# Attention followed by a gated feed-forward on one core: the loads of w3 and w_out first, four partial sums of their product held in the score buffers, dummy matmuls, and a new model and queue rule for the static order

## Chip, cores and metric

The kernel runs on one core of one Trainium2 chip. The metric is the device time of one execution in microseconds (us); lower is better. A time is about 1.7 us longer than the span that the profile of the same execution shows, so spans are compared with spans and times with times. TensorE is called PE below, ScalarE ACT, VectorE DVE, GpSimd POOL and SyncE SP, as the profile calls them.

## The reference

Sliding-window attention with four sink keys, then a multiplicative feed-forward without a nonlinearity:

```python
# q, k, v: [4 batches, 8 heads, 768 positions, 64];  n_sink 4, window 128
scores = q @ k.T / sqrt(64)
keep   = (key < 4) | (0 <= query - key < 128)
x      = softmax(where(keep, scores, -1e9)) @ v      # as [3072 tokens, 512]
a, b   = x @ w1, x @ w2                              # w1, w2: [512, 1024]
out    = ((a * b) @ w3) @ w_out                      # w3: [1024, 1024], w_out: [1024, 512]
```

All inputs are float32 in memory; the loads convert them to bfloat16 on the way.

## The kernel before

There is nothing nonlinear between `w3` and `w_out`, so the kernel multiplies them once ("the fold", `w3o = w3 @ w_out`) and then has only one product per token block. The fold needs 64 transposes of `w3` blocks and a product of 1024 x 1024 x 512. It uses nothing of q, k or v, so it can run while those are still being loaded.

All loads are issued by GpSimd, in one fixed order. `("w3", 2, 4)` is row blocks 2 and 3 of `w3`, `("wo", 0)` the left half of the columns of `w_out`, `("qkv", 0, 0, 2)` blocks 0 and 1 of k, q and v of batch 0:

```python
order = [("w3", 0, 1), ("wo", 0), ("w3", 1, 2), ("qkv", 0, 0, 2), ("w3", 2, 4), ("w1", 0), ("w2", 0),
         ("qkv", 0, 2, 4), ("wo", 1), ("w3", 4, 6), ("w1", 1), ("w2", 1), ("qkv", 0, 4, 6),
         ("w3", 6, 8), ("qkv", 1, 0, 6), ("qkv", 2, 0, 6), ("qkv", 3, 0, 6)]
# ... load(*order[0]), identity; then order[1:4]
# ... five affine_selects on GpSimd build the masks here
for x in order[4:]:
    load(*x)
```

The fold works by row block and half of the columns, so each matmul has 256 columns:

```python
def fold_mm(i, n):
    po = ps_mm.tile([P, DM // 2], FP32, tag="mm", name="pw")
    cols = slice(n * DM // 2, (n + 1) * DM // 2)
    for j in range(KFF):                          # KFF = 8
        nc.tensor.matmul(po[:], w3T[i][:, j, :], wo_sb[:, j, cols],
                         start=(j == 0), stop=(j == KFF - 1))
    yield
    nc.scalar.copy(w3o[:, i, cols], po[:])
```

The order of instructions on PE, ACT, DVE and SP is static. While the program is built, a small simulation decides it: it guesses when each load arrives, how long each task takes, and picks for each engine what to put next. Its guesses don't change what is computed, only the order in which each engine must do it:

```python
arrive, clock = {}, 2.2
def lands(key, us): ...                    # clock += us; arrive[key] = clock
# q, k, v block: 0.95 us each, and arrive + 3.0;  w3 row block: 1.5;  half of w1, w2, w_out: 3.0
...
URGENT = {"g": 0, "av": 0, "sc": 2}        # ACT and DVE: among what is ready, the most urgent first
```

Score tiles live in two buffers (`ps_sc`, `bufs=2`) of PSUM, the memory that PE writes its results to. Output tiles `o_sb` live in three SBUF buffers, and SP carries both the output stores and, for batches 2 and 3, the transposes of q and k by DMA.

The softmax here doesn't subtract the row's maximum and nothing guards it: scores larger than these inputs give would overflow.

## Time and profile before

| | before |
|---|---|
| time, median of the first three runs | 215.45 us (215.21 to 215.82) |
| span of the profiled run (its time 214.53 us) | 212.8 us |
| PE busy | 92% of the span |
| last fold matmul ends | 57.6 us |
| last of all weights and of batch 0 landed | 46.7 us |
| last load landed | 112.4 us |

The page of the profile gives busy time by engine, then the span in 40 equal slices with the busy share in tenths and the clock that was granted to PE, then the chain of waits followed back from the last instruction:

```profile
PE 195.3 (92%) x1888; PEld 131.8 (62%) x1888; DVE 109.5 (51%) x258; ACT 110.4 (52%) x197; POOL 75.0 (35%) x97
...
PE   0287799999998999999999999999999999999993
...
PEclk9999969999999999999999999999999999999998
...
PE 86%; POOL 5%; DMA 3%; DVE 3%; issue 1%; ACT 1%; POOLq 0%; ACTq 0%; DVEq 0%
```

PE is full from the sixth slice on. What is to be had lies in the first five slices (each 5.3 us), where PE shows 0, 2, 8, 7, 7 tenths. The view of waits says what PE waited for: total us, number of waits, longest:

```profile
PE tp_232 L301 <- DMA w_sb<-in_moe_w_dram: 5.1, 1, 5.1
PE pw L313 <- DMA wo_sb<-in_moe_w_out_dram: 3.8, 1, 3.8
PE tp_304 L301 <- DMA w_sb<-in_moe_w_dram: 1.4, 1, 1.4
PE xt L269 <- DVE xn L259: 1.2, 3, 0.6
```

The view by windows gives, for each stretch, its length and the busy time (with instruction count) of PE, PE's weight loads, DVE, ACT and POOL; then the granted clock, and two columns on DMA that are not used here:

```profile
0.00:10.00 10.00, 1.11 (x9) 0.95 (x10) 4.50 (x10) 1.28 (x1) 8.80 (x17) 1.00 0.85 110
10.00:20.00 10.00, 7.77 (x70) 6.22 (x71) 3.27 (x9) 1.33 (x3) 9.20 (x13) 1.00 1.75 183
20.00:30.00 10.00, 8.07 (x82) 5.55 (x77) 5.73 (x17) 5.58 (x10) 6.36 (x8) 0.86 1.90 178
30.00:37.00 7.00, 6.94 (x76) 5.76 (x75) 3.32 (x7) 3.54 (x8) 2.13 (x4) 0.95 1.22 207
37.00:60.00 23.00, 23.00 (x320) 20.51 (x316) 15.05 (x33) 13.78 (x29) 19.40 (x24) 1.00 2.27 163
60.00:85.00 25.00, 24.18 (x332) 19.92 (x333) 20.12 (x53) 17.51 (x33) 18.64 (x23) 1.00 2.21 149
```

Up to 37 us PE is busy for 1.11 + 7.77 + 8.07 + 6.94 = 23.9 us. The clock column needs care: before the first clock record it shows full speed. The first record in the trace, at 17.03 us, is the change *to* full speed. The durations agree with that. The timeline of PE lists start, length, instructions, and the idle time before them with what ended it:

```profile
5.07 1.03 PE L301 MATMUL tp_232<-ident,w_sb 128*128 128x128 bf16 x8 [5.07 <-DMA w_sb<-in_moe_w_dram]
9.92 1.87 PE L313 MATMUL pw<-wo_sb,w3t 128*128 128x256 bf16 x8 [3.82 <-DMA wo_sb<-in_moe_w_out_dram]
...
27.02 5.10 PE L284 MATMUL pg<-xT_102,w_sb 128*128 128x256 bf16 x30 [0.46 <-ACT xT_102 L271]
32.85 1.04 PE L313 MATMUL pw<-wo_sb,w3t 128*128 128x256 bf16 x8
```

Eight fold matmuls of one shape took 1.87 us at 9.92 us and 1.04 us at 32.85 us. The 30 gate matmuls at 27.02 us fell into a second stretch of half clock, recorded from 27.27 to 30.69 us.

### The profile page before, as it was taken

To read this page: it belongs to the slowest core of one execution; us is meant where nothing else is said; L and a number is where in the kernel's file an instruction comes from. 1 tells how busy PE (TensorE), PEld (TensorE's weight loads), DVE (VectorE), ACT (ScalarE), POOL (GpSimd) and SP (SyncE) were. 2 spreads that over 40 slices of the span, in tenths; PEclk is the share of its full clock that TensorE was granted. 3 is DMA by queue.
4 is the path that set the end of the run, shared out by engine and by line. 5 is a ranking of instruction groups with operands and counts; after the bars stand their busy time and mean duration, and the time that the engine had idled before them with its cause. 6 is when DMAs were issued, how large, how long until landed. Compare 5 with 4: busy or idle time off the path is not lost.

```text
span 212.8 us, 4647 instructions
## 1 busy us (share of the span) xinstructions
PE 195.3 (92%) x1888; PEld 131.8 (62%) x1888; DVE 109.5 (51%) x258; ACT 110.4 (52%) x197; POOL 75.0 (35%) x97
## 2 busy tenths in 40 slices
PE   0287799999998999999999999999999999999993
PEld 0266468998987887666666555666664466554441
DVE  7116825836697787776776444687740044440000
ACT  2012636644866686786666766766643333323332
POOL 7996573679999665666000000000000000000000
PEclk9999969999999999999999999999999999999998
DMA  4999999999999999999996222100002310002343
GB/s 65 160 170 205 165 198 204 163 178 157 156 155 132 156 156 149 136 154 146 140 117 124 102 107 93 49 2 3 0 3 99 148 49 3 2 0 99 152 162 133
DMA packets 96710, 24.43 MB, mean 115 GB/s; under 512 B 88496, under 2 KB 92592, under 8 KB 96688
## 3 DMA queue, kind: packets, MB, share of 16 engines
q0 software_dynamic: 80176, 14.69, 89.5%
q1 hardware_dynamic: 16512, 9.44, 21.3%
q8 instruction: 15, 0.25, 0.5%
q14 instruction: 7, 0.06, 0.1%
HBM read 29.36 MB, written 6.29 MB: 168 GB/s over the span
## 4 chain that ended last, share of the span: by engine, by line
PE 86%; POOL 5%; DMA 3%; DVE 3%; issue 1%; ACT 1%; POOLq 0%; ACTq 0%; DVEq 0%
PE pg L284 41%; PE po L323 20%; PE av L253 7%; PE sc L222 6%; PE pw L313 6%; DMA w_sb<-in_moe_w_dram 3%; PE xt L269 3%; PE sp L202 2%; PE tp L168 1%; POOL vN_90 L101 1%; POOL qN_82 L101 1%; DVE xn L259 1%; POOL kN_86 L101 1%; DVE am L231 1%; POOL w_sb L108 1%
## 5 line engine op out<-in xcount | busy, mean ns | idle before, releaser
L284 PEld LDWEIGHTS <-w_sb 128*128 128x128 bf16 x576 | 54.2, 99 | 27.6 <-issue 3.4
L227 ACT ACTIVATE ex<-sc 128x1024 bf16<-128x1024 f32 (+1 forms) x48 | 44.3, 955 | 13.3 <-PE sc L222 13.0
L291 ACT COPY a_sb<-pg 128x384 f32<-128x384 f32 (+1 forms) x72 | 32.1, 446 | 34.2 <-PE pg L284 20.0
L231 DVE TENSOR_TENSOR am<-ex,maskt 128x1024 bf16<-128x1024 bf16 (+1 forms) x48 | 30.4, 643 | 10.0 <-ACT ex L227 9.0
L327 ACT COPY o_sb<-po 128x512 f32<-128x512 f32 x24 | 14.0, 585 | 27.2 <-PE po L323 24.8
L284 PE MATMUL pg<-xT_102,w_sb 128*128 128x256 bf16 x192 | 26.6, 285 | 1.1 <-DVE kT_99 L171 0.6
L284 PE MATMUL pg<-xT_103,w_sb 128*128 128x384 bf16 x128 | 23.8, 326 | 0.0
L284 PE MATMUL pg<-xT_104,w_sb 128*128 128x384 bf16 x128 | 23.0, 326 | 0.0
L313 PE MATMUL pw<-wo_sb,w3t 128*128 128x256 bf16 x128 | 17.3, 291 | 4.6 <-DMA wo_sb<-in_moe_w_out_dram 3.8
L259 DVE TENSOR_TENSOR xn<-av,rec 128x256 bf16<-128x256 f32 x48 | 20.4, 425 | 1.7
L284 PE MATMUL pg<-xT_105,w_sb 128*128 128x384 bf16 x128 | 21.0, 326 | 0.0
L288 DVE TENSOR_TENSOR ab_109<-a_sb,pg 128x384 bf16<-128x384 f32 x16 | 8.9, 555 | 22.3 <-PE pg L284 22.3
L253 PEld LDWEIGHTS <-am 128*128 128x128 bf16 x352 | 16.7, 97 | 2.9 <-DVE am L231 1.1
L313 PEld LDWEIGHTS <-w3t 128*128 128x128 bf16 x128 | 12.5, 103 | 7.4 <-issue 3.1
L257 DVE RECIPROCAL rec<-av 128x4 f32<-128x4 f32 x48 | 8.6, 179 | 14.9 <-PE av L253 14.8
L316 ACT CAST w3o<-pw 128x256 bf16<-128x256 f32 x16 | 5.8, 379 | 18.0 <-PE pw L313 17.9
L288 DVE TENSOR_TENSOR ab_106<-a_sb,pg 128x256 bf16<-128x256 f32 x24 | 10.0, 417 | 9.7 <-PE pg L284 9.7
L288 DVE TENSOR_TENSOR ab_108<-a_sb,pg 128x384 bf16<-128x384 f32 x16 | 8.8, 552 | 5.8 <-PE pg L284 5.4
L323 PE MATMUL po<-w3o,ab_106 128*128 128x512 bf16 x48 | 11.4, 380 | 0.0
L269 PE MATMUL xt<-ident,xn 128*128 128x128 bf16 x96 | 9.7, 220 | 1.2 <-DVE xn L259 1.2
L323 PE MATMUL po<-w3o,ab_107 128*128 128x512 bf16 x48 | 10.7, 379 | 0.0
L323 PE MATMUL po<-w3o,ab_108 128*128 128x512 bf16 x48 | 10.7, 379 | 0.0
(129 smaller groups left out, 261.3 us busy)
## 6 DMA issues: line engine op xcount, KB each, us to landing
out_dram<-o_sb SPq DMA_DIRECT2D x24, 256.0 KB, 2.0
w_sb<-in_moe_w_dram POOLq DMA_DIRECT2D x7, 512.0 KB, 9.8
wo_sb<-in_moe_w_out_dram POOLq DMA_DIRECT2D x2, 512.0 KB, 8.8
kN_86<-in_k_dram POOLq DMA_DIRECT2D x6, 128.0 KB, 10.8
qN_82<-in_q_dram POOLq DMA_DIRECT2D x6, 128.0 KB, 10.7
vN_90<-in_v_dram POOLq DMA_DIRECT2D x6, 128.0 KB, 9.9
kN_87<-in_k_dram POOLq DMA_DIRECT2D x6, 128.0 KB, 7.2
qN_83<-in_q_dram POOLq DMA_DIRECT2D x6, 128.0 KB, 6.6
```

Of the source, the lines that this page charges most:

```text
L222: nc.tensor.matmul(sc[:, e, c:c + n], kT[b][hp, r, kb * P:(kb + 1) * P], qT[b][hp, r, qb * P:qb * P + n], start=True, stop=True)
L227: nc.scalar.activation(ex[:, :, c0:], sc[:, :, c0:], ACTF.Exp, scale=scale)
L231: nc.vector.tensor_mul(am[:, :, c0:], ex[:, :, c0:], mk)
L253: nc.tensor.matmul(o, lhs, rhs, start=(n == 0), stop=(n == len(todo) - 1), skip_group_check=True)
L259: nc.vector.tensor_mul(xn[:], av[:, :, :, 0:D], rec[:].to_broadcast([P, 2, 2, D]))
L269: nc.tensor.transpose(xt[:, r, i, :], xn[:, i, :, :].rearrange("p e d -> p (e d)"), ident[:])
L284: nc.tensor.matmul(pg[:], w_sb[:, kk, dt * P:(dt + 1) * P], xT[b][:, kk, tk], start=(kk == 0), stop=(kk == NP - 1))
L288: nc.vector.tensor_mul(ab[b][:, dt, tk], gate_a.pop((b, c, dt))[:], pg[:])
L291: nc.scalar.copy(a_sb[:], pg[:])
L313: nc.tensor.matmul(po[:], w3T[i][:, j, :], wo_sb[:, j, cols], start=(j == 0), stop=(j == KFF - 1))
L323: nc.tensor.matmul(po[:], ab[b][:, kk, m * P:(m + 1) * P], w3o[:, kk, :], start=(kk == 0), stop=(kk == KFF - 1))
L327: nc.scalar.copy(o_sb[:], po[:])
```

## The change

The intent is to give PE useful work while q, k and v are still on their way: load `w3` and `w_out` almost first, start the fold on half of `w_out`, fill what idle time is left with dummy matmuls that keep the clock up, and tell the scheduling model how loads really land, as one first-in-first-out queue.

Cut to its core (`...` marks cuts; in the last lines numbers from several lines are put into one, and the comments are mine):

```diff
+    SPLIT = 4
...
-    order = [("w3", 0, 1), ("wo", 0), ("w3", 1, 2), ("qkv", 0, 0, 2), ("w3", 2, 4), ("w1", 0), ("w2", 0),
-             ("qkv", 0, 2, 4), ("wo", 1), ("w3", 4, 6), ("w1", 1), ("w2", 1), ("qkv", 0, 4, 6), ...
+    order = [('w3', 2, 4, 1, 2), ('w3', 0, 1, 0, 1), ('w3', 1, 2, 0, 1), ('w3', 3, 4, 0, 1),
+             ('w3', 2, 3, 0, 1), ('wo', 0), ('w3', 0, 2, 1, 2), ('wo', 1), ('w3', 6, 8, 0, 2),
+             ('w3', 4, 5, 0, 2), ('qkv', 0, 0, 2), ('qkv', 0, 2, 4), ('w3', 5, 6, 0, 2), ('w1', 0),
+             ('w2', 0), ('w2', 1), ('w1', 1), ('qkv', 0, 4, 6), ('qkv', 1, 0, 6), ...
...
+    def fold_mm(i, j0, j1):
+        if i >= SPLIT:
+            po = ps_mm.tile([P, DM], FP32, tag="mm", name="pw")[:]
+        else:                                      # rows 0..3: held in the two score buffers
+            if i % 2 == 0 and j0 == 0:
+                held[i // 2] = ps_sc.tile([P, 2, DM], FP32, tag="sc", name="ph")
+            po = held[i // 2][:, i % 2, :]
+        for j in range(j0, j1):
+            nc.tensor.matmul(po, w3T[i][:, j, :], wo_sb[:, j, :],
                              start=(j == 0), stop=(j == KFF - 1))
...
+    def keep_busy(n):
+        pz = ps_mm.tile([P, 512], FP32, tag="mm", name="pz")
+        for _ in range(n):
+            nc.tensor.matmul(pz[:], idle[:, 0:P], idle[:, 0:512], start=True, stop=True)
...
-    clock = 2.2           # q/k/v 0.95 (+3.0 to arrive), w3 row block 1.5, other weights 3.0
+    LAG, clock = 1.5, 2.8 # q/k/v 0.87 (+0.75 beside DMA transposes), w3 half row block 0.64, others 2.57
+    XP_US = 7.5           # a DMA transpose, to landing; was 6.5
...
-    URGENT = {"g": 0, "av": 0, "sc": 2}               # rank among what is ready
+    YIELD = {"g": 0.0, "av": 0.0, "sc": 0.4}          # us that a task lets others go first
```

In the new order `w_out` is loaded by half of its rows, so a matmul of the fold has all 512 columns. The first four row blocks can accumulate over the first half of the inner dimension as soon as the first half of `w_out` is there, and finish with the second half. In between, their partial sums stay in the two score buffers.

## The prediction

> **What bounds the kernel now.** TensorE. The busy table gives PE 92% of the 212.8 us span (ScalarE 52%, VectorE 51%); the chain of waits is 86% PE. By windows, PE is nearly full from 31 us to 209 us. The loss is the start: in 0:35 us PE is busy 21.9 us, part of it at half clock. The waits view gives 5.1 us until the first w3 block lands, 3.8 us for w_out's first half, 1.4 us for w3 blocks 2 and 3. The clock records show half speed until 17.0 us and again from 27.3 to 30.7 us (32 gate matmuls there took 5.8 us; at the later pace of 109 ns they take 3.5).
>
> The loads are a queue that never empties: they land in the order of issue, 2.5 us apart per 512 KB of weights and 0.87 us per 128 KB of q, k or v, until all weights and batch 0 are in at 46.7 us. The change moves the same bytes, so that moment stays; only what PE does meanwhile can change.
>
> **What the change does.**
> 1. It loads w3 and w_out almost first. 3 MB (15 us of queue) buys 64 transposes (56 ns each) and all fold matmuls.
> 2. Fold matmuls are 64 of 512 columns, not 128 of 256: by the projection's pace (216 ns against 110 ns) 13.8 us instead of 14.1. Four row blocks accumulate half by half in the score buffers, so they start on half of w_out. PSUM copies: 8 of 0.59 us instead of 16 of 0.38; off the chain.
> 3. 29 dummy matmuls fill idle time and warm the clock. The Trainium skill ("TensorE: Matmul & The Clock Gate", Part 1) says the clock is throttled until about 3.4 us of activity; this trace agrees that it is half until 17.0 us of sparse work.
> 4. The fold ends early, so projections of batch 0 become a stock of ready PE work.
>
> **Cost.** The first four small loads are followed on GpSimd by four mask operations (about 2.4 us in this trace), so the queue should run dry for about 2 us around 6 to 8 us. I estimate w_out's halves landing near 12.2 and 16 us, batch 0's second key pair at 30 us, the first gate weights complete near 37 us. By then the changed kernel will have done about 23.7 us of useful PE work (fold 17.4, attention of two blocks 6.3); the kernel before had done about 17.0. With the fold's 0.3 us that is a lead of about 7 us. Part goes back: the third block of q and k lands about 3 us later than before (44 to 47 us), and the changed order asks for it near 44 us; I expect 1.5 to 2.5 us of load waits in 40 to 62 us. Before lost about 4 us after 37 us; I expect much the same in total. After 62 us PE should be full, with the same 40 us tail.
>
> **Predicted time: 208.3 us** (205.0 to 212.0). Faster by over 2%: 0.82; within 2%: 0.16; slower: 0.02.
>
> **What would show it.** Clock full from 5 to 7 us on, with no second dip; PE waiting on w_out near 12 us; last fold matmul near 35 us (before 57 us); gates starting near 37 us; load waits on kN and qN near 44 us; spacing of loads unchanged; PE over 97% busy from 62 us on.
>
> **What would make it wrong.** Faster if the dry spell does not occur (all lands 1.5 us earlier). Slower if output stores and transposes collide with batch 2 and 3 loads, or if the static order makes PE wait on ScalarE or VectorE after 60 us.

## The result

The changed kernel takes 209.68 us (median of four runs, 209.37 to 209.99); the kernel before takes 215.33 us in its four runs (214.63 to 215.82). The ratio is 0.974, with a 95% interval from 0.971 to 0.977. Ratios are the mean time of one kernel's fast runs over that of the other's of the same rounds, so not quite the ratio of the medians. The result is correct. On one core a run counts as slow when it is over 1.5% above the fastest of the same kernel.

The spans of the two profiled runs are 212.8 and 208.3 us. They are 4.5 us apart where the medians are 5.65 us apart, because the profiled run of before was a fast one (214.53 us) and that of after its slowest (209.99 us).

The page and the chain of waits after, as shown of before:

```profile
PE 197.4 (95%) x1841; PEld 125.1 (60%) x1853; DVE 110.2 (53%) x262; ACT 110.3 (53%) x189; POOL 77.0 (37%) x101
...
PE   7968988999999999999999999999999999999993
...
PEclk9999999999999999999999999999999999999999
...
PE 72%; DMA 18%; POOL 6%; issue 2%; ACT 1%; POOLq 0%; ACTq 0%
```

Here the slices mislead, since dummies count as busy PE. DMA's share of the chain rose from 3% to 18% while the time fell: the chain now runs back through the loads of the start. A share of a chain is not a loss. The waits of PE after:

```profile
PE ph L327 <- DMA wo_sb<-in_moe_w_out_dram: 2.5, 2, 2.0
PE pz L352 <- DVE ksbd_113 L135: 1.3, 1, 1.3
...
PE tp L176 <- DMA kN_86<-in_k_dram: 0.4, 1, 0.4
PE tp L176 <- DMA qN_82<-in_q_dram: 0.3, 1, 0.3
```

The timeline of PE after, at the places that the argument needs (`pz` is a dummy, `ph` a held partial sum):

```profile
1.33 6.58 PE L352 MATMUL pz<-ksbd_113 128*128 128x512 bf16 x19 [1.33 <-DVE ksbd_113 L135]
...
9.71 2.11 PE L352 MATMUL pz<-ksbd_113 128*128 128x512 bf16 x8
13.83 3.61 PE L327 MATMUL ph<-wo_sb,w3t 128*128 128x512 bf16 x16 [2.00 <-DMA wo_sb<-in_moe_w_out_dram]
...
36.27 1.90 PE L327 MATMUL pw<-wo_sb,w3t 128*128 128x512 bf16 x7
```

The windows after:

```profile
0.00:10.00 10.00, 8.22 (x45) 3.96 (x46) 5.60 (x15) 1.28 (x1) 8.79 (x19) 1.00 0.61 82
10.00:20.00 10.00, 7.41 (x40) 3.52 (x40) 1.51 (x8) 0.52 (x1) 6.17 (x9) 1.00 1.14 186
20.00:30.00 10.00, 9.29 (x83) 5.47 (x84) 3.50 (x6) 4.38 (x9) 7.18 (x9) 1.00 2.29 159
30.00:37.00 7.00, 5.97 (x79) 3.99 (x79) 5.89 (x15) 4.42 (x7) 5.34 (x8) 1.00 1.45 198
37.00:60.00 23.00, 22.76 (x297) 18.80 (x296) 16.93 (x40) 14.73 (x28) 17.63 (x23) 1.00 2.15 168
60.00:85.00 25.00, 24.84 (x302) 18.75 (x303) 18.04 (x47) 17.84 (x32) 18.39 (x23) 1.00 2.15 150
```

The clock is at full speed from 6.04 us on and does not dip again until the very end. The last fold matmul ends at 38.2 us instead of 57.6 us. The gates start at 40.0 us instead of 26 us: the changed kernel does the fold first and the gates later.

### Counting useful work, not busy time

Because busy PE includes dummies and slow matmuls, I use a count that includes neither. Each matmul of the program is given the start-to-start time that it has in undisturbed stretches of these traces (56 ns for 128 columns, 109 ns for 256, 216 ns for 512), and a dummy is given zero. These are the intervals of the Trainium skill, "TensorE: Matmul & The Clock Gate", section "Wait — 56ns, not 53.3ns?" (columns divided by 2.4 GHz, plus about 2.5 ns), and the trace agrees: the 16 `ph` matmuls above took 3.61 us, of which the last one's modelled length is 0.38, so 15 intervals of 215 ns. The sum over the program is 185.0 us before and 184.9 us after. (How the small and the overlapping matmuls of the attention are counted moves the sum: recounts gave 181 to 187 us. It moved the leads below by at most 0.4 us.) The *lead* of a kernel at a moment is the useful work that before still has to do at that moment, less what the kernel still has to do. At the end of the execution it is the difference of the spans.

| lead over before, us, at | 20 us | 37 us | 60 us | 90 us | 105 us | 150 us |
|---|---|---|---|---|---|---|
| after | 2.0 | 4.5 | 3.5 | 5.4 | 4.8 | 4.5 |

By 37 us before had done 16.7 us of useful work and after 21.1 us. The same count gives the PE time without useful work in each stretch:

| PE time without useful work, us | 0 to 37 | 37 to 60 | 60 to 85 | 85 to 105 | from 105 |
|---|---|---|---|---|---|
| before | 20.3 | 0.4 | 2.4 | 0.5 | 0.3 |
| after | 15.9 | 1.4 | 0.5 | 1.0 | 0.6 |

So the gain of 4.5 us of span is a gain of 4.4 us in the first 37 us, 1.0 us given back up to 60 us, 1.9 us gained between 60 and 85 us, and 0.8 us given back after that.

### The profile page after: what moved, and what is told of

The parts are those of the page before. It is cut to its first block, busy times and chain, and to the rows that moved or that the text cites. A ratio compares the mean times of both kernels' runs of the same rounds, so it can differ in the third digit from the quotient of the medians.

```text
span 208.3 us, 4575 instructions
## 1 busy us (share of the span) xinstructions
PE 197.4 (95%) x1841; PEld 125.1 (60%) x1853; DVE 110.2 (53%) x262; ACT 110.3 (53%) x189; POOL 77.0 (37%) x101
## 4 chain that ended last, share of the span: by engine, by line
PE 72%; DMA 18%; POOL 6%; issue 2%; ACT 1%; POOLq 0%; ACTq 0%
PE pg L292 36%; PE po L338 20%; PE av L261 6%; DMA w_sb<-in_moe_w_dram 6%; DMA wo_sb<-in_moe_w_out_dram 5%; PE sc L230 5%; DMA vN_90<-in_v_dram 5%; DMA qN_83<-in_q_dram 3%; PE xt L277 2%; POOL w_sb L109 2%; PE sp L210 1%; PE tp L176 1%; POOL w_sb L105 1%; POOL sel L154 1%; POOL vN_91 L102 0%
## 5 line engine op out<-in xcount | busy, mean ns | idle before, releaser
L292 PEld LDWEIGHTS <-w_sb 128*128 128x128 bf16 x576 | 53.1, 98 | 24.0 <-issue 1.4
L235 ACT ACTIVATE ex<-sc 128x1024 bf16<-128x1024 f32 (+1 forms) x48 | 45.0, 956 | 8.0 <-PE sc L230 7.9
L292 PE MATMUL pg<-xT_102,w_sb 128*128 128x256 bf16 x192 | 24.3, 273 | 0.0
L296 DVE TENSOR_TENSOR ab_109<-a_sb,pg 128x384 bf16<-128x384 f32 x16 | 8.9, 555 | 19.0 <-PE pg L292 19.0
L265 DVE RECIPROCAL rec<-av 128x4 f32<-128x4 f32 x48 | 8.6, 180 | 16.7 <-PE av L261 16.4
L331 ACT CAST w3o<-ph 128x512 bf16<-128x512 f32 x4 | 2.2, 587 | 18.8 <-PE ph L327 18.5
L327 PEld LDWEIGHTS <-w3t 128*128 128x128 bf16 x64 | 6.0, 98 | 9.8 <-issue 2.9
L338 PE MATMUL po<-w3o,ab_106 128*128 128x512 bf16 x44 | 11.0, 379 | 0.2
L338 PE MATMUL po<-w3o,ab_107 128*128 128x512 bf16 x46 | 10.9, 379 | 0.1
L338 PE MATMUL po<-w3o,ab_108 128*128 128x512 bf16 x47 | 10.6, 379 | 0.1
L338 PE MATMUL po<-w3o,ab_109 128*128 128x512 bf16 x47 | 10.5, 379 | 0.1
L296 DVE TENSOR_TENSOR ab_107<-a_sb,pg 128x384 bf16<-128x384 f32 x16 | 8.9, 553 | 3.0 <-PE pg L292 2.0
L296 DVE TENSOR_TENSOR ab_108<-a_sb,pg 128x384 bf16<-128x384 f32 x16 | 8.9, 554 | 2.9 <-PE pg L292 2.1
```

Of the source, the lines that this page charges most:

```text
L235: nc.scalar.activation(ex[:, :, c0:], sc[:, :, c0:], ACTF.Exp, scale=scale)
L265: nc.vector.reciprocal(rec[:], av[:, :, :, D:D + 1])
L292: nc.tensor.matmul(pg[:], w_sb[:, kk, dt * P:(dt + 1) * P], xT[b][:, kk, tk], start=(kk == 0), stop=(kk == NP - 1))
L296: nc.vector.tensor_mul(ab[b][:, dt, tk], gate_a.pop((b, c, dt))[:], pg[:])
L327: nc.tensor.matmul(po, w3T[i][:, j, :], wo_sb[:, j, :], start=(j == 0), stop=(j == KFF - 1))
L338: nc.tensor.matmul(po[:], ab[b][:, kk, m * P:(m + 1) * P], w3o[:, kk, :], start=(kk == 0), stop=(kk == KFF - 1))
```

## The experiments

The theory: the gain is useful PE work done while loads are on their way, made possible by the new order of loads *together with* the held partial sums; it was smaller than predicted because the loads of the start landed later than estimated. Rivals: (a) the gain is the clock, kept up by the dummies; (b) the gain is the scheduling model and the queue rule, and the order of loads matters little.

Twelve kernels ran, all with correct results, in three batches, each batch on one chip beside runs of the kernel before. The median of before was 215.92, 215.71 and 215.81 us in the batches (lowest 214.24, highest 217.54). Unless said otherwise, the edit is to the changed kernel.

| run | time, us (lowest to highest) | ratio to before [95%] | lead at 37 us | lead at 90 us | lead at 150 us |
|---|---|---|---|---|---|
| e1_early_loads | 207.83 (207.31 to 209.09) | 0.965 [0.958, 0.972] | 6.2 | 7.1 | 6.9 |
| e2_no_dummies | 209.20 (208.90 to 210.64) | 0.972 [0.965, 0.979] | 4.9 | 5.8 | 5.6 |
| e3_no_held | 213.18 (211.76 to 213.88) | 0.990 [0.982, 0.998] | 2.8 | 3.0 | 2.9 |
| e4_before_dummies | 215.68 (214.74 to 216.69) | 1.001 [0.994, 1.008] | 0.9 | 0.9 | -0.2 |
| e5_old_order | 221.92 (220.12 to 222.57) | 1.028 [1.022, 1.035] | -4.2 | -5.9 | -6.8 |
| e6_old_queues | 216.68 (215.13 to 218.76) | 1.003 [0.995, 1.011] | 3.7 | 1.6 | -4.2 |
| e7_old_model | 219.92 (219.75 to 220.19) | 1.020 [1.015, 1.026] | 3.8 | 4.7 | -5.4 |
| e8_early_no_dummies | 209.84 (207.86 to 210.87) | 0.973 [0.965, 0.980] | 5.9 | 5.9 | 4.2 |
| e9_old_model_7buf | 210.65 (210.39 to 211.08) | 0.975 [0.971, 0.980] | 3.5 | 4.4 | 4.2 |
| e10_old_queues_late_sv | 214.39 (214.00 to 214.52) | 0.992 [0.987, 0.997] | 4.3 | 2.0 | 0.1 |
| e11_after_again | 209.66 (208.97 to 210.72) | 0.971 [0.967, 0.975] | 4.9 | 5.7 | 5.5 |
| e12_best | 207.38 (207.08 to 207.97) | 0.960 [0.957, 0.964] | 6.7 | 7.3 | 7.4 |

The leads are those of the one profiled run of each kernel (a slow one for e6), so a few tenths of a us mean nothing: e11 is the changed kernel once more, in another batch and on another chip than the first two batches, and its lead at 37 us is 0.4 us above that of the first profile.

### e1: all of the first eight loads ahead of the masks

```diff
-    for x in order[1:4]:
+    for x in order[1:8]:
         load(*x)
     # ... masks on GpSimd ...
-    for x in order[4:]:
+    for x in order[8:]:
```

> The changed kernel, with the loads of the first eight pieces (up to the second half of w_out) issued before the four mask operations on GpSimd; instruction order on TensorE is unchanged. Theory A (the shortfall against the prediction is the load queue's dry spell while GpSimd makes the masks): w_out's halves land near 11.5 and 15.5 us instead of 13.8 and 18.4, everything after it lands about 2 us earlier, and the time falls by 1.5 to 2 us, to about 208 us. Rival (the late start is the DMA engines' own ramp-up, or descriptor writing held up by VectorE): landings move by less than 0.7 us and the time stays within 0.5 us of 209.7.

The time is 207.83 us, 1.85 us less than the changed kernel's 209.68. The order of instructions on PE is identical. The two halves of `w_out` landed at 11.98 and 16.41 us; in the changed kernel it was 13.78 and 18.38 us. The timeline of GpSimd in the changed kernel shows why:

```profile
3.04 1.12 POOL L109 DMA_DIRECT2D w_sb<-in_moe_w_dram  x2
4.15 0.67 POOL L145 TENSOR_SCALAR_AFFINE_SELECT maskt<-maskt 128x512 bf16<-128x512 bf16 x1
...
5.35 1.10 POOL L154 TENSOR_SCALAR_AFFINE_SELECT sel<-sel 4x1024 bf16<-4x1024 bf16 x1
...
6.57 0.57 POOL L109 DMA_DIRECT2D w_sb<-in_moe_w_dram  x1
```

From 4.15 to 6.57 us GpSimd makes masks and issues nothing, and the queue later runs almost dry: from 9 to 10 us it moved 14 to 17 KB in each half microsecond, where about 100 KB is usual, and e1 moved 99 and 100 KB there. (A smaller dip near 5.5 us, 25 KB, is in e1 too, with 36 KB.) PE's first fold matmuls in e1:

```profile
12.03 3.61 PE L327 MATMUL ph<-wo_sb,w3t 128*128 128x512 bf16 x16 [0.16 <-DMA wo_sb<-in_moe_w_out_dram]
```

The intervals of the two ratios just touch (0.972 here, 0.971 for the changed kernel), so the time alone would not settle it. The landings do: over all runs of the new order with the masks first the halves came at 13.19 to 14.52 and 17.82 to 18.60 us, in the three with the early loads (e1, e8, e12) at 11.98 to 12.39 and 15.93 to 17.19 us. The Trainium skill, "GPSIMD Engine Reference", section "When to use GPSIMD", says that it is cores of this engine that write the descriptors of such loads; this trace shows the consequence, that its compute and its loads stand in one line.

### e2: without the dummies

```diff
-                if gap > 0.5 and start < WARM_UNTIL and rings["mm"][0][0] is not None \
+                if False and gap > 0.5 and start < WARM_UNTIL and rings["mm"][0][0] is not None \
```

> The changed kernel without the 29 dummy matmuls; the order of all other work is the same. Theory A (the gain is real work done while loads arrive, the clock only helps): the fold's first 16 matmuls run at half clock and end near 20.5 us instead of 17.3, the clock rises there, and the kernel loses 1 to 2.5 us, to about 211 us, still clearly faster than 215.3. Rival B (the warm clock is most of the gain): the time goes back to 213 us or more.

Not as I expected: the time is 209.20 us, no worse than with the dummies. The clock was at half speed until 17.34 us instead of 6.04. The first 16 fold matmuls show it, in the timeline of PE:

```profile
13.26 5.61 PE L327 MATMUL ph<-wo_sb,w3t 128*128 128x512 bf16 x16 [3.10 <-DMA wo_sb<-in_moe_w_out_dram]
```

They took 5.61 us, against 3.61. At 20 us the lead is 1.2 us against 2.0, but at 37 us it is 4.9 against 4.5. The second half of `w_out`, and then k and q, were what PE had to wait for, so 2 us of slow matmuls shortened later waits by as much. (The halves of `w_out` also landed 0.6 us earlier in this profile, at 13.22 and 17.82 us, which is within the scatter of such runs.) Rival (a) falls here.

### e4: the dummies alone, in the kernel before

```diff
+    idle = ksbd[B - 1]
+    nc.vector.memset(idle[:], 0.0)
...
+    def keep_busy(n): ...          # as in the change, and the rule that calls it
```

> The kernel before with the dummy matmuls alone added by the same rule, nothing else changed. Theory A: the clock is full from 6 us and does not dip at 27 us; the early fold matmuls are waiting for data anyway, so only the dip's 1.7 us and under 1 us of the start come back: 213 to 214 us. Rival B (the clock is most of the gain): 211.5 us or less.

The ratio is 1.0005. The clock was full from 3.98 us, half again from 10.81 to 14.22 us, and full after that; the dip at 27 us is gone. The lead was 0.9 us from 37 to 90 us, and a wait of 1.0 us on a transposed q (at 93.9 us) took it back. So a better clock gained less than 1 us in that kernel too, and one wait 50 us later spent it.

### e3: without the held partial sums

```diff
-    SPLIT = 4
+    SPLIT = 0
```

> The changed kernel with no row block accumulated half by half (all eight fold products wait for the whole of w_out, in the ordinary buffers). If the held partial sums are what lets the fold begin early, the first fold matmul starts near 18.5 us instead of 13.8 and PE has done 3 to 3.5 us less by 25 us; part comes back since the loads of batch 0 limit PE later (it has spare time to catch up near 25 to 33 us): 1 to 3 us lost, 211 to 212.5 us. If the held sums do not matter: 210 us or less.

The time is 213.18 us: 3.5 us of the gain is gone. The first fold matmul started at 17.76 us, shortly before the second half of `w_out` landed (18.38 us), instead of 13.83 us, right after the first half:

```profile
17.76 7.07 PE L327 MATMUL pw<-wo_sb,w3t 128*128 128x512 bf16 x32
```

The lead at 20 us is -0.8 us instead of 2.0, and at 37 us 2.8 us instead of 4.5.

### e5: the held partial sums with the old order of loads

```diff
-    order = [('w3', 2, 4, 1, 2), ('w3', 0, 1, 0, 1), ...
+    order = [("w3", 0, 1, 0, 2), ("wo", 0), ("w3", 1, 2, 0, 2), ("qkv", 0, 0, 2), ("w3", 2, 4, 0, 2), ("w1", 0),
+             ("w2", 0), ("qkv", 0, 2, 4), ("wo", 1), ...     # the old sequence; w_out by halves of its rows
```

> Everything of the change kept (held partial sums, wide fold matmuls, dummies, FIFO load model, new rule for ScalarE and VectorE queues), but the loads in the old order, with w_out by row halves and w3 by whole row blocks. Theory A (the order of loads, so what PE can do while they come, is the gain): PE has done about as little by 37 us as in the kernel before (17 us of work instead of 22), and the time is 213.5 to 216 us. Rival C (the scheduling rules and model are the gain): 211 us or less.

The time is 221.92 us, 2.8% slower than before. Two lines of its PE timeline say why:

```profile
21.94 5.56 PE L350 MATMUL pz<-ksbd 128*128 128x512 bf16 x25
...
32.04 2.75 PE L325 MATMUL ph<-wo_sb,w3t 128*128 128x512 bf16 x12 [0.26 <-DMA wo_sb<-in_moe_w_out_dram]
```

The partial sums occupy both score buffers, and until the second half of `w_out` lands (32 us in this order) they cannot be finished. So the attention, whose q and k were transposed at 16 us, could not start (its first scores came at 38.3 us), and PE ran 25 dummies instead. The held sums are a gain only if the second half of `w_out` comes soon after the first. Together with e3, this shows that the two parts are not two gains that add up: the held sums need the new order, and the new order without them has 2.8 of the 4.5 us of lead at 37 us. The old order without held sums, under the new model and rule, was not run.

### e7: the old model of the loads, the same loads

```diff
-    LAG = 1.5
-    clock = 2.8
+    clock = 2.2
...
-                    lands(0.87, (n, i[0], kb))
+                    lands(0.95, (n, i[0], kb)) ; arrive[n, i[0], kb] += 3.0
-            lands(0.64 * ...)   # w3
+            lands(0.75 * ...)
-            lands(2.57, (what, i[0]))
+            lands(3.0, (what, i[0]))
-    XP_US = 7.5
+    XP_US = 6.5
```

> The changed kernel with only the old arrival times in the scheduler's load model (slower weights, q, k, v 3 us late); the loads themselves are the same. It changes PE's order: it does all of the fold of rows 0 to 3 and 6, 7 and 4 before the first q and k. Theory A: small, since the work is there in either order: 209.5 to 211 us. Rival C (the better model is what keeps PE full): 212 us or more, with waits on loads between 24 and 45 us doubled from about 1.5 us.

The time is 219.92 us, 10 us more than with the new model. The lead was 3.8 us at 37 us and 4.7 us at 90 us, almost that of the changed kernel. All was lost in one wait, in the view of waits:

```profile
PE xt L277 <- ACT o_sb L342: 7.4, 1, 7.4
```

PE waited for a PSUM buffer that ACT had to empty first. The timelines of ACT and of SP lead further back:

```profile
87.84 0.59 ACT L279 COPY xT<-xt 128x512 bf16<-128x512 bf16 x1
98.02 0.58 ACT L342 COPY o_sb<-po 128x512 f32<-128x512 f32 x1 [9.59 <-DMA out_dram<-o_sb]
```

```profile
88.92 1.26 SPq L185 DMA_TRANSPOSE qT<-qN  x1
90.27 8.69 SPq L345 DMA_DIRECT2D out_dram<-o_sb  x4
```

ACT could not write an output tile because all three `o_sb` buffers still held tiles that were not stored. Their stores stood on SP behind twelve DMA transposes, which SP issued one after the other from 70.0 to 90.2 us. In the changed kernel SP issues eight transposes, a store, two more, a store, one more, a store and so on in this stretch, so the stores get away from 81 us on.

PE's clock also fell, from 93.76 to 104.0 us. The Trainium skill ("TensorE: Matmul & The Clock Gate", Part 1) says that an idle window of about 3.4 us throttles the clock. Here the record of the fall comes 2.5 us after the last matmul before the wait (91.3 us), so a little less idle time was enough; the half-speed stretch of 10.24 us is three such windows long. It adds to the wait, since PE worked at half speed from 98.7 to 104.0 us.

### e9: the old model again, with seven output buffers

`w3t` (used in the fold only) and `o_sb` (used later) have the same size, so they can share one set of seven buffers where they had four and three:

```diff
-            w3T[i] = work.tile([P, KFF, P], BF16, tag="w3t", bufs=4, name="w3t")
+            w3T[i] = work.tile([P, KFF, P], BF16, tag="w3t", bufs=7, name="w3t")
-        o_sb = work.tile([P, DM], FP32, tag="o_sb", name="o_sb")
+        o_sb = work.tile([P, DM], FP32, tag="w3t", bufs=7, name="o_sb")
```

> The kernel with the old load model again, in the very same order on every engine, but output tiles share the seven buffers of the fold's transposed rows and of the output (before: three for outputs, four for the fold). Theory D (its loss is one 7.4 us wait near 91 us: ScalarE needs an output buffer, the stores that would free one stand behind twelve transposes in SyncE's queue): the wait goes, and with it the half clock of 94 to 104 us, so the time falls from 219.9 to 209 to 212 us. If the stores only slow the loads, the time stays above 215 us.

The time is 210.65 us, 9.3 us less than e7. The order of instructions is the same as e7's on every engine; only the buffers differ. The window from 85 to 105 us, first of e7:

```profile
85.00:105.00 20.00, 12.58 (x101) 7.20 (x98) 6.10 (x14) 7.55 (x12) 9.66 (x12) 0.74 1.86 175
```

and then of e9:

```profile
85.00:105.00 20.00, 19.95 (x215) 12.97 (x213) 13.14 (x33) 15.20 (x27) 9.80 (x13) 1.00 1.85 176
```

SP still issues its twelve transposes in a row, and the stores still leave late (at 91.8 us). With seven buffers nobody waits for them, and the clock stays up. That settles the cause of e7, and it says what the new model is worth here: not a gain of its own, but an order in which the stores are not late. With enough buffers the difference between the models is 1.0 us (210.65 against 209.66 in the same batch, with intervals of the ratios that overlap); the new model with seven buffers alone was not run.

### e6: the old rule for the queues of ACT and DVE

```diff
-    YIELD = {"g": 0.0, "av": 0.0, "sc": 0.4}
+    URGENT = {"g": 0, "av": 0, "sc": 2}
     # ... and the old choice: among what is ready, the lowest rank first
```

> The changed kernel with only the old rule for the order of ScalarE's and VectorE's work (strict urgency classes). Theory A: start-up is the same until about 33 us, the time moves by at most 1.5 us from the changed kernel (210 to 211.2 us), since PE is full anyway. Rival C: over 212.5 us.

The median is 216.68 us. One of the four runs, the profiled one (218.76 us), counts as slow and is left out of the ratio; the median of the other three is 215.52 us, so the rule is worth about 6 us, which is all of the gain: without it the changed kernel is no faster than before. Its lead at 37 us, 3.7 us, is nearly there all the same; it is lost later. Whatever is read from the trace of the slow run is only a lead to follow, and e10 was made to test it. The one large wait in that trace:

```profile
97.29 0.41 PE L200 MATMUL vp<-vN,sel 128*128 128x64 bf16 x8 [3.83 <-DMA vN<-in_v_dram]
```

Here PE waits for the first v block of batch 3, which landed at 97.24 us. In the changed kernel it landed at 93.19 us. The rule changes the order of all engines a little, and with it the moment at which buffers of batch 1 come free, and with that the order in which GpSimd issues the loads of batch 3.

### e10: as e6, with this one wait taken away

```diff
-                     [("av", b - 2, NP - 1, NT - 1)] if b >= 2 else [], [("v", b, 0)], "mm")
+                     ([("av", b - 2, NP - 1, NT - 1)] if b >= 2 else [])
+                     + ([("sc", b, 3, 0)] if b == 3 else []), [("v", b, 0)], "mm")
```

PE takes up the sink values of batch 3 only after that batch's first scores.

> The kernel with the old queue rule again, with one order changed: TensorE does the sink values of batch 3 only after that batch's first scores, so that it does not wait on the first v block of batch 3 (that wait was 3.8 us near 94 us, and 1.7 us of half clock follow). If this wait is the loss of that kernel: 210.5 to 212.5 us. If the old rule costs in many small waits: 214 us or more.

The time is 214.39 us. That is 1.1 us less than the median of e6's fast runs, or 2.4 us less by the ratios to before, so the wait on v seems to be a part of what the old rule costs, but the smaller one (the intervals of the two ratios still overlap, 0.995 to 0.997): 4.7 us remain against e11 in the same batch. The leads say where: e10 has 4.3 us at 37 us, 1.0 us at 60 us and 2.0 us at 90 us; the changed kernel has 4.5, 3.5 and 5.4. So 2.3 us more are lost between 37 and 60 us. The windows view of e10 confirms an idle PE there (20.54 us busy of 23, against 22.76 in the changed kernel):

```profile
37.00:60.00 23.00, 20.54 (x257) 16.30 (x257) 15.61 (x36) 12.88 (x24) 16.53 (x20) 1.00 2.16 167
```

Of that, 1.7 us are two waits on k and 0.7 us two waits on q; later there is one of 1.4 us on a transposed q. Why this order asks for them too early while the other does not was not settled.

e6 and e10 also decide what is left of rival (b). The lead at 37 us is there under the old rule (3.7 and 4.3 us, against 4.5) and under the old model (3.8 us in e7, 3.5 in e9), so the order of loads and the held sums make most of it. Keeping it to the end took the new rule. The new rule alone in the kernel before was not run. That kernel lost 3.6 us after 37 us, and a rule that left its start as it is could win back no more than that.

### e8: e1 and e2 together

The edits of e1 and e2 in one kernel.

> Early loads as in the first experiment, without the dummies. If the half clock of the first 17 us is paid back by waits for data around 24 to 34 us, as in the run without dummies, this equals the early-load kernel (207.3 to 208.3 us); if early data leaves PE no wait to absorb it, it costs 1 to 2 us (209 us).

The time is 209.84 us, but the four runs scatter from 207.86 to 210.87, so this settles little. In the profiled run (210.34 us) the half clock of the start is not what is missing: the lead at 37 us is 5.9 us, close to e1's 6.2. It lost 1.7 us from there on, with waits of 2.3 us in total on blocks of v.

### e11 and e12: the changed kernel again, and a better one

e12 joins the early loads of e1, the shared seven buffers of e9 and the late sink values of e10, in the changed kernel with its new model and rule.

> The changed kernel itself once more, beside the others on one chip: 0.974 of the kernel before as in its first timing, within 0.006, with no wait of PE over 2.5 us after 20 us.

> The changed kernel with all three remedies: eight loads ahead of the mask operations, seven shared output buffers, batch 3's sink values late. In the early-load run the time was 207.8 us; the buffers and the late sink values take away the waits that showed up near 90 us in some runs of the sister kernels, so its runs should scatter less: 206.5 to 208 us, 0.96 of before, all runs within 1 us.

The changed kernel came out as before, at 209.66 us. e12 takes 207.38 us (six runs, 207.08 to 207.97), the best of all: ratio to before 0.960. Its lead grows from 6.7 us at 37 us to 7.4 us at the end. Once PE has begun, no single wait of it is longer than 0.6 us. What each of the three remedies adds was not separated here.

## Why the prediction was right, and where its terms were off

**The time and the mechanism were right.** 208.3 us was predicted, with a range from 205 to 212; 209.68 us was measured. The gain comes where it was said to come from: 4.4 us of the 4.5 us of span are useful PE work done before 37 us. e3 and e5 show that the whole lead takes the new order and the held sums together; e2 and e4 show that it is not the clock. What the prediction does not have is the price of losing the lead again: it does not mention the queue rule, and without that rule (e6) the gain is gone by the end.

**The lead at 37 us was over-sized: about 7 us predicted, 4.5 us measured.** The failed term is "By then the changed kernel will have done about 23.7 us of useful PE work"; it had done 21.1 us (before: 16.7, predicted 17.0). What was wrong in it were the landing times. The halves of `w_out` were estimated at 12.2 and 16 us and landed at 13.78 and 18.38 us; the rest followed with a shift of 2 us or so. The dry spell itself was sized right: about 2 us predicted, and e1, which removes it, brings the halves 1.8 and 2.0 us forward and the time down 1.85 us. What was missed is the start. The first load, of the same 256 KB as before's first, took 5.18 us from issue to landing instead of 3.71, so that it landed at 6.50 us and not at 5.02. I had taken over before's start. It is not the dummies: without them it landed at 6.28 us, still 1.3 us late. Nor is it the held sums, the new model or the rule: e5 has all of them, but the old order of loads, and there the first load landed at 5.07 us. In all runs with the old first load (one row block, written in pieces of 2 KB: before, e4, e5) it landed at 5.02 to 5.16 us, in all with the new one (two half row blocks, pieces of 1 KB) at 6.03 to 7.24 us. So the new order of loads does it, by the form of its first load or by what is queued behind it; which of the two was not separated.

**The give-back was over-sized as well.** 1.5 to 2.5 us of load waits were predicted between 40 and 62 us, on the third block of k and q near 44 us. PE lost 1.0 us more than before in 37 to 60 us, and no wait on k or q was left in that stretch. The block came no earlier than forecast (45.27 to 48.75 us); but since all else was late too, PE took it up only at 47.77 us.

**The kernel before lost 3.6 us after 37 us, where about 4 us were predicted, and after lost 3.5 us.** "Much the same in total" holds, though not in the same places: before lost 2.4 us between 60 and 85 us, after 0.5 us. With the old queue rule (e6, e10) the lead grew by 0.8 and 1.0 us from 60 to 90 us; with the new one by 1.9 to 2.2 us in after, e7 and e9, but by only 1.6 us in e3 and 1.3 us in e5. So the rule may have a part in this gain, as far as single profiles can say.

**The clock was right, its worth was not.** Full clock "from 5 to 7 us on, with no second dip" was predicted, and it was 6.04 us without a dip. Here the skill ("TensorE: Matmul & The Clock Gate", Part 1: about 3.4 us of activity, depending on the phase of the window) was a rough guide: the dummies began at 1.33 us, so it took 4.7 us, and between 2.7 us (e4) and 5.8 us (e5) in other runs. That no second dip came was in part luck: in the profile of e6, with the same dummies at the start, PE was idle for 2.13 us before the first `ph` matmuls (2.00 us in the changed kernel), and the clock was half again from 15.71 to 19.13 us. And the prediction named the clock among the losses of the start without asking what it is worth while loads are the limit. By e2 it is worth nothing that these runs can resolve.

**The danger was named, and it is real.** The prediction said "Slower if output stores and transposes collide with batch 2 and 3 loads". In the changed kernel the loads between 75 and 98 us did come 1.9 us apart instead of 0.87, while SP's transposes were under way; that agrees with the Trainium skill, "DMA: Bandwidth & Descriptors", section "Issuing engines are not separate DMA queues". The collision that costs, however, is on SP's own queue (e7, e9): stores behind transposes, three output buffers, 9.3 us.

**What stays open:** what in the new order makes the first load land 1.5 us later; what the new queue rule would do alone in the kernel before; and the 4.7 us by which e10 trails the changed kernel: its waits on k and q after 37 us come to 4.0 us (1.7 + 0.7 + 0.2 + 1.4), but the step by which the queue rule brings them about was not found.

## What to carry to other kernels

When a kernel starts by waiting for its data, look for work that depends on the fewest bytes, load those bytes first, and count what the engine does usefully by a given moment; busy time and the clock did not tell the gain here, the useful work did. A partial sum that is held while its second operand comes is a loan of its buffer: with the operand soon behind it gained 3.5 us, with the operand late it cost more than the whole change gained. After a change of order, look at what an in-order queue carries behind what, since stores behind twelve transposes took nearly twice what the change had brought (10.2 us), and four more output buffers gave 9.3 us of it back. And a lead at the start is no gain yet: under the old queue rule it was lost before the end.

## What the Trainium skill lacked or had wrong

- "TensorE: Matmul & The Clock Gate", section "Back-to-back issue gap", gives a sustained spacing of about 81 ns for 128 columns and about 131 ns for 512 columns in a stream of weight loads and matmuls, and calls N/2.4 + 2.5 ns the gap of an isolated one. Here such streams ran at 215 ns for 512 columns (16 `ph` matmuls, each with its weights) and 56 ns for 128 columns (eight transposes in 0.61 us, of which the last one's modelled length is 0.22). The formula held and the two sustained figures did not.
- "DMA: Bandwidth & Descriptors", section "Anatomy of one DMA — SWDGE (gpsimd) path", has 2.0 us plus bytes at 436 GB/s, which is an estimate of 3.2 us for the first load (512 KB of float32 read, 256 KB of bfloat16 written). It took 3.71 us from issue to landing in one kernel and 5.18 us in the other; over all runs 3.7 to 3.9 us where it is written in pieces of 2 KB and 4.7 to 5.9 us where in pieces of 1 KB, with another load behind it.
- The same page does not say which bytes count where a load converts. Half of a weight matrix (1 MB read, 512 KB written) landed every 2.5 us: 419 GB/s of what is read, close to the page's 436, and 210 GB/s of what is written. Blocks of q, k and v, written in pieces of 128 bytes, came at 256 KB read per 0.87 us, 301 GB/s. That they are slower agrees with the line in "Specifications" that asks for 512 bytes; a figure to plan with is lacking.
- No page that I found says outright that compute on GpSimd holds up the loads that it issues: issuing eight loads instead of four before 2.4 us of masks went with 1.85 us less of the whole kernel (e1).
- "DMA: Bandwidth & Descriptors" gives DMA transposes a bandwidth, but no time on the queue that issues them, except in a part on trn3. SP spent 1.2 to 3.3 us on each in these runs; in e7 twelve in a row took 20 us, and the stores behind them were issued only from 90.3 us on.
- "TensorE: Matmul & The Clock Gate", Part 1, treats the warm-up as a loss. No page says that it may be hidden: with 11 us more of half clock at the start (until 17.34 us instead of 6.04) the kernel took 209.20 us, with the dummies 209.68 us (e2).
